# Linear attention and a gated expert on one core: the feature projections from split fp32r products to plain fp32 ones

## The chip, the cores and the metric

The kernel runs on one core of a Trainium2 chip. The metric is the device time of one execution in microseconds, the median of several runs. Before the change it is 1270.08 us (three runs, 1269.09 to 1270.28).

## The reference

```python
def phi(x):                                   # x: 8 batches, 8 heads, 576 rows, 64
    proj = np.einsum('bhsd,df->bhsf', x, w_phi)            # w_phi: 64 x 128
    proj = proj - np.max(np.abs(proj), axis=-1, keepdims=True)
    return np.concatenate([np.exp(proj), np.exp(-proj)], axis=-1)
q_p, k_p = (phi(q), phi(k))
kv = np.einsum('bhsf,bhsd->bhfd', k_p, v)
z = np.sum(k_p, axis=2)
num = np.einsum('bhsf,bhfd->bhsd', q_p, kv)
den = np.einsum('bhsf,bhf->bhs', q_p, z)[..., None] + 1e-06
attn = num / den                              # then x = 4608 tokens x 512
rms = np.sqrt(np.mean(x * x, axis=-1, keepdims=True) + 1e-06)
xn = x / rms * rms_g
g = xn @ w_gate                               # 512 x 1536
out = (g * (1.0 / (1.0 + np.exp(-g))) * (xn @ w_val)) @ w_out
```

The change concerns the first product alone, `proj`, for q and for k.

## The kernel before

The work is done in stages that follow each other. The attention stage takes the 64 heads in 32 pairs (8 batches of 4 pairs). Behind it come the gate and value products of the first 384 columns that are left over, then the other gate and value columns, then the product with `w_out`. Nearly all products are made in fp32 accuracy from three fp32r ones: each operand is split into a rounded high part (a cast on ScalarE) and the rest (a subtraction on VectorE or GpSimd), and high x high, high x low and low x high are added up in PSUM. `_split` (line 59) issues the cast and the subtraction.

A pair goes through four steps, each in another turn of the loop at line 558, so that four pairs are in work at a time:

- `front` (line 316) transposes k, q and the rests on TensorE and projects them. A head has 576 rows; 512 of them fill four blocks of 128, and the remaining 64 rows of k and of q of both heads form one more block of 128 rows, the rests, called `r`. Two of a head's blocks lie side by side in 128 columns (64 each), so a pair has four units of 128 x 128 for k, four for q and one for the rests. `trans` (line 324) transposes the units of one of them into a PSUM tile `sm` and splits the result into `th` and `tl`. `proj` (line 334) takes two units: for each it issues three products (lines 341 to 343) of a unit with the weights `wh` and `wl`, 128 x 256. These hold the split `w_phi` twice, in rows 0 to 63 for the first 128 columns and in rows 64 to 127 for the others, and zeros elsewhere, so that one product projects both blocks of a unit. VectorE then takes the largest absolute value of each projected row (line 345) and subtracts it (line 348), which gives `yk`, `yq` and `yr`. The PSUM tile `pp` holds two units (one bank) and has two buffers.
- `mid` (line 355) takes the exponentials of k's part (line 368), sums k's features times v in `acc` (lines 376 and 381), transposes q's part back (line 394), takes its exponentials twice, plain and rounded (lines 405 and 406), and subtracts them on GpSimd (lines 410 and 412).
- `back` (line 430) multiplies q's features with the sums (line 445), copies numerator and denominator out on ScalarE (line 447), and sends the denominators through DRAM to spread them (lines 449 to 458).
- `last` (line 468) multiplies with the reciprocals on VectorE (lines 475 and 476) and stores.

In the same loop the weights of the later stages are decoded from 8-byte numbers (`_decode`, line 41: four instructions on VectorE, two on ScalarE, two on GpSimd), and from the pair on at which enough tokens are stored, units of the gate and value products fill TensorE (`fill`, line 494, products at line 511).

`_merge` (line 64) orders the steps' pieces by a place between 0 and 1 in the turn; `front`'s pieces are spread from -0.2 to 0.7 in the order that line 352 gives. The framework's scheduler then sets the final order on each engine. Every engine runs its own queue in that order and waits at semaphores.

## Time and profile before

| | |
|---|---|
| median of the runs | 1270.08 us |
| the profiled execution | 1266.87 us, span 1265.1 us |
| TensorE busy | 1221.9 us, 97%, 10401 products |
| VectorE busy | 963.8 us, 76% |
| ScalarE busy | 738.1 us, 58% |
| GpSimd busy | 684.5 us, 54% |
| granted TensorE clock, mean | 0.999 |
| attention stage | 0 to about 487 us |
| rest of the first gate and value columns | to about 590 us |
| other gate and value columns | to about 1000 us |
| product with `w_out` | to the end |

The names in the trace are those of the tiles: `pp<-wh,th` is a product into `pp` with the operands `wh` and `th`. PE is TensorE, PEld its weight loads, DVE VectorE, ACT ScalarE, POOL GpSimd. A product's row lasts longer than the time until the next one may start, so that rows of one engine overlap.

### The profile page before, as it was taken

Reading aid. Unit: us, or ns where it says so; the run is one execution under the profiler, and the core shown is the slowest. Engines: PE = TensorE matmul, PEld = TensorE weight load, DVE = VectorE, ACT = ScalarE, POOL = GpSimd, SP = SyncE. Lnnn points to the kernel's source line nnn. Section 1 sums busy time; section 2 is a strip of 40 time slices with the busy share of each in tenths; the row PEclk is TensorE's granted clock in tenths of the full one; section 3 lists DMA queues with packets and bytes.
Section 4 is the critical chain, followed back from the end, with each engine's and each line's share of the span. In section 5 each row is a group of like instructions: output and inputs, shape, how many; then the busy total and the mean of one; then the engine's idle time right before and its main releaser. Section 6 shows DMA issues by size and latency. Waiting matters only on the chain.

```text
span 1265.1 us, 27382 instructions
## 1 busy us (share of the span) xinstructions
PE 1221.9 (97%) x10401; PEld 1206.2 (95%) x10401; DVE 963.8 (76%) x1425; ACT 738.1 (58%) x1514; POOL 684.5 (54%) x638
## 2 busy tenths in 40 slices
PE   7989999989999999999999999999999899999998
PEld 7989999989999999999999999999999799999998
DVE  6999898987778663574867877877775888877775
ACT  6988887887888775454545445444345534344342
POOL 4766664774666455226234444533431067877776
PEclk9999999999999999999999999999999999999999
DMA  5555665666575425764445545556665653544443
GB/s 162 138 139 152 172 164 168 167 164 171 161 185 157 138 73 164 239 210 146 144 145 201 171 161 185 193 179 214 220 201 192 207 162 108 180 136 135 134 145 106
DMA packets 196977, 208.37 MB, mean 165 GB/s; under 512 B 67722, under 2 KB 148270, under 8 KB 196846
## 3 DMA queue, kind: packets, MB, share of 16 engines
q1 hardware_dynamic: 175982, 186.17, 49.4%
q10 hardware_dynamic: 20864, 20.45, 5.2%
q8 instruction: 82, 1.34, 0.5%
q14 instruction: 49, 0.40, 0.1%
HBM read 133.91 MB, written 72.67 MB: 163 GB/s over the span
## 4 chain that ended last, share of the span: by engine, by line
PE 69%; DVE 15%; DMA 5%; ACT 4%; issue 4%; POOL 1%; ACTq 0%; SPq 0%; DVEq 0%; POOLq 0%
PE r L786 20%; PE fp L511 8%; PE gz L1030 6%; PE gd L1030 5%; PE gy L1030 5%; PE acc L381 5%; PE sm L445 3%; PE fp L1030 3%; PE sm L511 2%; PE pp L341 2%; PE pp L343 2%; PE pp L342 2%; PE sm L328 2%; PE fp L445 2%; PE sm L394 2%
## 5 line engine op out<-in xcount | busy, mean ns | idle before, releaser
L786 PE MATMUL r<-xo,wh 128*128 128x256 f32 x1764 | 306.9, 278 | 4.9 <-ACT c L797 1.6
L786 PEld LDWEIGHTS r<-xo,wh 128*128 128x128 f32 x1764 | 264.7, 188 | 6.6 <-ACT c L797 1.8
L410 POOL TENSOR_TENSOR ql<-eq,qh 128x256 fp32r<-128x256 f32 x256 | 213.8, 865 | 60.2 <-ACT qh L406 40.5
L786 PE MATMUL r<-xo,wl 128*128 128x256 f32 x882 | 239.2, 277 | 0.0
L786 PEld LDWEIGHTS r<-xo,wl 128*128 128x128 f32 x882 | 164.0, 188 | 0.0
L345 DVE TENSOR_REDUCE mx<-pp 128x4 f32<-128x512 f32 (+1 forms) x160 | 99.8, 629 | 49.8 <-PE pp L343 49.1
L381 PE MATMUL acc<-vm,ek 128*128 128x65 f32 x1024 | 129.9, 268 | 0.0
L381 PEld LDWEIGHTS acc<-vm,ek 128*128 128x128 f32 x1024 | 126.2, 192 | 0.1
L406 ACT ACTIVATE qh<-sm 128x512 fp32r<-128x512 f32 (+1 forms) x192 | 97.5, 508 | 0.0
L405 ACT ACTIVATE eq<-sm 128x512 f32<-128x512 f32 x128 | 78.8, 616 | 28.3 <-PE sm L394 24.9
L341 PE MATMUL pp<-wh,th 128*128 128x256 f32 x288 | 88.5, 308 | 3.3 <-DVE yk L348 1.2
L343 PE MATMUL pp<-wh,tl 128*128 128x256 f32 x288 | 84.7, 300 | 0.4 <-DVE tl L61 0.3
L61 POOL TENSOR_TENSOR xo<-x,xo 128x512 fp32r<-128x512 f32 x45 | 64.0, 1429 | 33.8 <-ACT xo L60 31.4
L342 PE MATMUL pp<-wl,th 128*128 128x256 f32 x288 | 81.6, 284 | 0.0
L368 ACT ACTIVATE ek<-yk 128x512 f32<-128x512 f32 x128 | 75.3, 655 | 1.0 <-DVE yk L348 0.9
L807 ACT ACTIVATE c<-c 128x1024 f32<-128x1024 f32 (+1 forms) x45 | 44.0, 977 | 52.2 <-DVE c L806 52.2
L511 PE MATMUL fp<-xoh,fg 128*128 128x256 f32 x344 | 71.7, 287 | 1.2 <-ACT sums L169 1.2
L511 PE MATMUL fp<-xoh,fv 128*128 128x256 f32 x344 | 71.7, 284 | 0.0
L61 POOL TENSOR_TENSOR s2l<-st,s2h 128x768 fp32r<-128x768 f32 x17 | 39.7, 2337 | 54.1 <-ACT s2h L60 50.8
L54 POOL TENSOR_TENSOR stg<-stg,stg 128x128 f32<-128x128 f32 x48 | 24.5, 531 | 78.6 <-ACT c L803 35.2
L412 POOL TENSOR_TENSOR ql<-eqr,qh 128x256 fp32r<-128x256 f32 x32 | 24.5, 765 | 76.8 <-ACT qh L406 76.8
L54 POOL TENSOR_TENSOR wa<-raw,wa 128x192 f32<-128x192 f32 x64 | 41.7, 672 | 43.8 <-DVE wa L52 18.2
(262 smaller groups left out, 4157.2 us busy)
## 6 DMA issues: line engine op xcount, KB each, us to landing
ht<-hs SPq DMA_DIRECT2D x17, 1536.0 KB
hs<-c SPq DMA_DIRECT2D x36, 512.0 KB
gvr<-gvs SPq DMA_DIRECT2D x27, 512.0 KB
rc<-di SPq DMA_DIRECT2D x32, 288.0 KB
x<-xs SPq DMA_DIRECT2D x9, 1024.0 KB
gvs<-fo ACTq DMA_DIRECT2D x35, 256.0 KB
kt<-in_k_dram SPq DMA_DIRECT2D x32, 256.0 KB
vm<-in_v_dram SPq DMA_DIRECT2D x64, 128.0 KB
```

Source lines behind the costliest of these rows:

```text
L61: (lo_eng or nc.vector).tensor_tensor(lo, x, hi.bitcast(F32), ALU.subtract)
L341: nc.tensor.matmul(o, th[:, cs], wh, start=True, stop=False)
L342: nc.tensor.matmul(o, th[:, cs], wl, start=False, stop=False)
L343: nc.tensor.matmul(o, tl[:, cs], wh, start=False, stop=True)
L345: nc.vector.tensor_reduce(mx[:, 0:2 * m], pp[:, 0:2 * m], axis=AX.X, op=ALU.max, apply_absolute_value=True)
L381: nc.tensor.matmul(acc[:, sg, h], e[h][:, sg, j], vm[:, h, j], start=False, stop=(h == 1 and j == T0 - 1))
L405: nc.scalar.activation(ei[:, sg], yi, AF.Exp, scale=1.0 - 2.0 * sg)
L406: nc.scalar.activation(hi[:, sg], yi, AF.Exp, scale=1.0 - 2.0 * sg)
L410: nc.gpsimd.tensor_tensor(lo[:, sg, cs], ei[:, sg, cs], hi[:, sg, cs].bitcast(F32), ALU.subtract)
L511: nc.tensor.matmul(fp[:, wi], w, xx[x][:, c], start=(wi == 0 and i == 0), stop=(i == 3 * NC - 1), skip_group_check=True)
L786: nc.tensor.matmul(self.r[r][:, k], w[:, cs], x[:, h, c], start=(first and k == 0 and i == 0), stop=(i == 3 * NP1 - 1), skip_group_check=True)
L1030: nc.tensor.matmul(place[n], a[:, kp], w[:, o], start=(first and kp == 0 and i == 0), stop=(kp == KP - 1 and i == 2), skip_group_check=True)
```

## The change

`w_phi` is kept once, unsplit, as `wphi` (`w2` in the code), in the same block form. `trans` makes one plain fp32 copy `th` of the transposed data, on VectorE for q and on ScalarE for k and the rests; `tl` is gone. `proj` does all units of k or of q in one piece. For k and q each unit becomes two products of 64 rows: rows 0 to 63 of the unit with rows 0 to 63 of the weights, and rows 64 to 127 with rows 64 to 127, 128 columns each, so that the zero blocks aren't multiplied; the built program gives the two their own halves of TensorE's rows. The first half's results go to one PSUM bank and the second half's to another; `pp` now holds four units in two banks and has one buffer. The rests have one plain product of 128 rows and 256 columns, into a `sm` tile. The reduction and the subtraction on VectorE take all four units at once (1024 elements a row), and `y` is written in the order that `mid` reads. Line 352's order has two pieces for each of k, q and r where it had up to three.

The matter of how many instructions a pair issues: on TensorE 27 products become 17; on VectorE two subtractions of 512 and one of 128 elements become one copy of 512, four reductions and four subtractions of 512 become two and two of 1024; on ScalarE one cast of 512 goes. GpSimd's work and the DMAs are the same.

```diff
--- before.py
+++ after.py
@@ -228,17 +228,14 @@
     ld = a_ctx.enter_context(tc.tile_pool(name="a_ld", bufs=2))
     dec = a_ctx.enter_context(tc.tile_pool(name="a_dec", bufs=1))
     dsc = a_ctx.enter_context(tc.tile_pool(name="a_dsc", bufs=3, space=DRAM))
-    ps_p = a_ctx.enter_context(tc.tile_pool(name="a_ps_p", bufs=2, space=PSUM))
+    ps_p = a_ctx.enter_context(tc.tile_pool(name="a_ps_p", bufs=1, space=PSUM))
     ps_k = a_ctx.enter_context(tc.tile_pool(name="a_ps_k", bufs=1, space=PSUM))
 
 
-    wh = const.tile([128, 2 * F], F32R, name="wh")
-    wl = const.tile([128, 2 * F], F32R, name="wl")
-    w2 = dec.tile([128, 2, F], F32, name="wa", bufs=2)
+    w2 = const.tile([128, 2, F], F32, name="wphi")
     nc.vector.memset(w2, 0.0)
-    nc.sync.dma_start(out=w2[0:64, 0, :], in_=w_phi)
-    nc.sync.dma_start(out=w2[64:128, 1, :], in_=w_phi)
-    _split(nc, wh, wl, w2[:, 0:2].rearrange("p a f -> p (a f)"))
+    for i in range(2):
+        nc.sync.dma_start(out=w2[i * 64:(i + 1) * 64, i], in_=w_phi)
 
 
     vms = [const.tile([128, 2, T0, D + 1], F32, name=f"vm{i}") for i in range(3)]
@@ -326,31 +323,34 @@
             tp = ps_s.tile([128, 512], F32, name="sm")
             for j, u in enumerate(us[n]):
                 nc.tensor.transpose(out=tp[:, j * 128:(j + 1) * 128], in_=u, identity=ident)
-            th = wk.tile([128, 512], F32R, name="th")
-            tl = wk.tile([128, 512], F32R, name="tl")
-            _split(nc, th[:, 0:m], tl[:, 0:m], tp[:, 0:m])
-            hl[n] = (th, tl)
-
-        def proj(n, u0):
-            th, tl = hl[n]
-            m = min(2, len(us[n]) - u0)
-            pp = ps_p.tile([128, 4, F], F32, name="pp")
-            for j in range(m):
-                o = pp[:, 2 * j:2 * j + 2].rearrange("p a f -> p (a f)")
-                cs = slice((u0 + j) * 128, (u0 + j + 1) * 128)
-                nc.tensor.matmul(o, th[:, cs], wh, start=True, stop=False)
-                nc.tensor.matmul(o, th[:, cs], wl, start=False, stop=False)
-                nc.tensor.matmul(o, tl[:, cs], wh, start=False, stop=True)
-            mx = wk.tile([128, 4], F32, name="mx")
-            nc.vector.tensor_reduce(mx[:, 0:2 * m], pp[:, 0:2 * m], axis=AX.X, op=ALU.max,
-                                    apply_absolute_value=True)
-            y = wk.tile([128, 4 if n != "r" else 2, F], F32, name="y" + n, bufs=3 if n != "r" else 2)
-            nc.vector.tensor_tensor(y[:, 0:2 * m], pp[:, 0:2 * m],
-                                    mx[:, 0:2 * m].unsqueeze(2).broadcast_to([128, 2 * m, F]), ALU.subtract)
-            d["y"][n, u0 // 2] = y
-
-        order = "k k0 r r0 k2 q q0 q2" if pr == 0 else "r k r0 k0 q k2 q0 q2"
-        return [lambda s=s: proj(s[0], int(s[1])) if s[1:] else trans(s) for s in order.split()]
+            hl[n] = wk.tile([128, 512], F32, name="th")
+            (nc.vector.tensor_copy if n == "q" else nc.scalar.copy)(hl[n][:, 0:m], tp[:, 0:m])
+
+        def proj(n):
+            th, m = hl[n], len(us[n])
+            if n == "r":
+                pp = ps_s.tile([128, 512], F32, name="sm")[:, 0:2 * F].rearrange("p (i m f) -> p i m f", i=2, m=1)
+                nc.tensor.matmul(pp.rearrange("p i m f -> p (i m f)"), th[:, 0:128],
+                                 w2.rearrange("p i f -> p (i f)"), start=True, stop=True)
+            else:
+                pp = ps_p.tile([128, 2, 4, F], F32, name="pp")
+                for j in range(m):
+                    for i in range(2):
+                        ps = slice(i * 64, (i + 1) * 64)
+                        nc.tensor.matmul(pp[:, i, j], th[ps, j * 128:(j + 1) * 128], w2[ps, i], start=True, stop=True)
+            mx = wk.tile([128, 2, 4], F32, name="mx")
+            nc.vector.tensor_reduce(mx[:, :, 0:m], pp, axis=AX.X, op=ALU.max, apply_absolute_value=True)
+            y = wk.tile([128, 2 * m, F], F32, name="y" + n)
+            nc.vector.tensor_tensor(y.rearrange("p (m i) f -> p i m f", i=2), pp,
+                                    mx[:, :, 0:m].unsqueeze(3).broadcast_to([128, 2, m, F]), ALU.subtract)
+            if n == "r":
+                d["y"]["r", 0] = y
+            else:
+                for h in range(2):
+                    d["y"][n, h] = y[:, 4 * h:4 * h + 4]
+
+        order = "k pk r pr q pq" if pr == 0 else "r k pr pk q pq"
+        return [lambda s=s: proj(s[1]) if s[1:] else trans(s) for s in order.split()]
 
     def mid(pr):
         d = st[pr]
```

TensorE, one pair of the attention stage, from the transposes of `mid` (`yq`) to those of q (`qt`). Before:

```order
L394 MATMUL sm<-ident,yq 128x128 x4
L341 MATMUL pp<-wh,th 128x256
L342 MATMUL pp<-wl,th 128x256
L343 MATMUL pp<-wh,tl 128x256
L341 MATMUL pp<-wh,th 128x256
L342 MATMUL pp<-wl,th 128x256
L328 MATMUL sm<-ident,qt 128x128 x4
```

The two units' products stand three to a unit; that of the second unit's low part (line 343) follows further down, since it waits for the split. Now, at the same place (line 325 is the transposes, 333 the rests' product, 340 the half products):

```order
L394 MATMUL sm<-ident,yq 128x128 x4
L333 MATMUL sm<-wphi,th 128x256
L340 MATMUL pp<-wphi,th 128x128 x8
L445 MATMUL fp<-qh,kv0h 65x288
L445 MATMUL fp<-ql,kv0h 65x288
L445 MATMUL fp<-qh,kv0l 65x288
```

The eight half products of k stand in one run, the rests' product ahead of them; products of `back` (line 445) follow, and q's transposes behind these.

VectorE, the same steps: the largest values (`mx`), the subtractions (`yk`, `yq`), the split (`tl`) and the decoding (`wp`). Before:

```order
L345 TENSOR_REDUCE mx<-pp 128x4
L61 TENSOR_TENSOR tl<-sm,th 128x512
L348 TENSOR_TENSOR yk<-pp,mx 128x512
L345 TENSOR_REDUCE mx<-pp 128x4
L348 TENSOR_TENSOR yk<-pp,mx 128x512
L50 TENSOR_SCALAR wp<-wa 128x384
L345 TENSOR_REDUCE mx<-pp 128x4
L51 SCALAR_TENSOR_TENSOR wp<-wa,wp 128x384
L348 TENSOR_TENSOR yq<-pp,mx 128x512
```

A reduction of one buffer stands between the subtractions of the other. Now (line 327 is q's copy, 342 the reduction, 344 the subtraction):

```order
L342 TENSOR_REDUCE mx<-sm 128x2
L344 TENSOR_TENSOR yr<-sm,mx 128x256
L342 TENSOR_REDUCE mx<-pp 128x8
L344 TENSOR_TENSOR yk<-pp,mx 128x2x4x128
L327 COPY th<-sm 128x512
L342 TENSOR_REDUCE mx<-pp 128x8
L50 TENSOR_SCALAR wp<-wa 128x384
L344 TENSOR_TENSOR yq<-pp,mx 128x2x4x128
```

There is one reduction and one subtraction each; between k's subtraction and q's reduction stands only q's copy.

## Rows read from the trace of the kernel before

**Rows 1.** The page, part 1: busy time, share and instructions of each engine.

```profile
span 1265.1 us, 27382 instructions
PE 1221.9 (97%) x10401; PEld 1206.2 (95%) x10401; DVE 963.8 (76%) x1425; ACT 738.1 (58%) x1514; POOL 684.5 (54%) x638
```

**Rows 2.** Table by stretches: engines' busy us and instruction counts, clock, DMA.

```profile
0.00:320.00 320.00, 297.88 (x2452) 290.53 (x2453) 274.06 (x496) 259.72 (x635) 196.90 (x262) 0.99 0.61 159
320.00:487.00 167.00, 166.36 (x1420) 165.50 (x1420) 118.60 (x202) 130.72 (x311) 101.18 (x122) 1.00 0.51 139
487.00:590.00 103.00, 100.29 (x859) 99.52 (x858) 55.45 (x76) 52.91 (x88) 45.09 (x35) 1.00 0.61 197
```

**Rows 3.** The same table for the projections' first products alone, line L341.

```profile
0.00:320.00 320.00, 62.93 (x201) 38.94 (x201) 0.99 0.61 159
320.00:487.00 167.00, 25.52 (x87) 16.53 (x87) 1.00 0.51 139
```

**Rows 4.** Chain of waits, in order of time: start, us, what.

```profile
204.47 0.28 PE acc L376 x2
204.74 0.44 PE sm L328 x4
...
213.37 0.12 PE pp L341
...
213.96 0.12 PE pp L343
...
215.22 0.22 PE acc L376 x2
```

**Rows 5.** Chain of waits from 0 to 487 us, shares by line.

```profile
by line: PE acc L381 13.0%; PE fp L511 10.5%; PE sm L445 8.6%; PE pp L341 4.7%; PE pp L343 4.7%; PE pp L342 4.3%; PE sm L328 4.3%; PE fp L445 4.3%; PE sm L394 4.2%; DVE mx L345 4.2%; issue 2.6%; DVE nd L476 2.4%; DVE yq L348 2.3%; PE acc L3
```

**Rows 6.** One of TensorE's weight loads, beside the six products of rows 4.

```profile
213.45 0.19 PEld L341 LDWEIGHTS pp<-wh,th 128*128 128x128 f32 x1
```

**Rows 7.** Groups of TensorE's instructions from 0 to 487 us, shapes apart.

```profile
L394 PE MATMUL sm<-ident,yq 128*128 128x128 f32 x256 | 39.4, 274 | 5.6 <-DVE tl L61 4.7 <-DVE yq L348 0.7
```

**Rows 8.** The same for VectorE: count, busy us, mean ns, idle before.

```profile
L345 DVE TENSOR_REDUCE mx<-pp 128x4 f32<-128x512 f32 x128 | 86.8, 684 | 42.6 <-PE pp L343 41.9
L348 DVE TENSOR_TENSOR yk<-pp,mx 128x512 f32<-128x512 f32 x64 | 43.8, 686 | 1.2
L61 DVE TENSOR_TENSOR tl<-sm,th 128x512 fp32r<-128x512 f32 x64 | 43.4, 678 | 9.8 <-ACT th L60 9.7
L348 DVE TENSOR_TENSOR yr<-pp,mx 128x256 f32<-128x256 f32 x32 | 13.3, 417 | 0.5
L345 DVE TENSOR_REDUCE mx<-pp 128x2 f32<-128x256 f32 x32 | 13.2, 413 | 7.2 <-PE pp L343 7.2
L61 DVE TENSOR_TENSOR tl<-sm,th 128x128 fp32r<-128x128 f32 x32 | 8.5, 264 | 0.6 <-ACT th L60 0.4
```

**Rows 9.** VectorE's copies out of PSUM in the stretch from 487 to 590 us.

```profile
L516 DVE COPY fo<-fp 128x512 f32<-128x512 f32 x6 | 4.1, 681 | 1.5 <-PE fp L511 1.5
```

**Rows 10.** ScalarE's casts of transposed data, groups from 0 to 487 us.

```profile
L60 ACT CAST th<-sm 128x512 fp32r<-128x512 f32 x64 | 38.9, 608 | 13.9 <-PE sm L328 10.5 <-PE pp L342 2.1 <-PE fp L445 1.0
```

**Rows 11.** ScalarE in order of time: two of 0.6 us, one after the other.

```profile
473.09 0.60 ACT L405 ACTIVATE eq<-sm 128x512 f32<-128x512 f32 x1
473.59 0.59 ACT L406 ACTIVATE qh<-sm 128x512 fp32r<-128x512 f32 x1
```

**Rows 12.** Who waited for whom from 0 to 487 us: total, times, longest.

```profile
DVE mx L345 <- PE pp L343: 49.1, 41, 4.2
PEld sm L394 <- DVE tl L61: 5.9, 6, 2.2
PE sm L394 <- DVE tl L61: 4.7, 5, 2.0
```

**Rows 13.** TensorE in order of time, in the first microseconds.

```profile
14.77 0.64 PE L376 MATMUL acc<-vr,er 128*128 128x130 f32 x2
15.21 0.32 PE L381 MATMUL acc<-vm,ek 128*128 128x65 f32 x1
```

## Prediction

> **What bounds the kernel now.** I read the busy shares first: TensorE 97%, VectorE 76% [rows 1]. A matmul's row is longer than its share of the queue, so a busy share doesn't say that TensorE is at its limit; the table by stretches does, since it counts instructions. It splits the span into the attention stage (0 to 487 us), the rest of the gate and value products (to 590), and two stages that the change doesn't touch (to 1265) [rows 2]. All 288 first products of the projections lie in the attention stage, 201 of them before 320 us and 87 after it [rows 3]. A pair of heads issues nine, so these are 22.3 pairs in 320 us (14.35 us each) and 9.7 pairs in 167 us (17.2 us each). I call them stages A and B.
>
> What a product costs TensorE is the distance to the next start in the chain of waits: six of the projection follow each other, and from the first's start at 213.37 us to the sixth's at 213.96 are 0.59 us, 0.118 each [rows 4]. By that, the 2452 products of stage A need 289 us, or 13.0 us a pair, and the 1420 of stage B all of its 167 us. **Stage B is bound by TensorE alone**: VectorE has 118.6 us to do there and ScalarE 130.7. **Stage A has three nearly level engines**: TensorE 13.0 us a pair, VectorE 274.1/22.3 = 12.3, ScalarE 259.7/22.3 = 11.6. The period is 14.35, so waiting for each other costs 1.35 us a pair. The chain over the whole stage agrees: the projection's three lines hold 4.7 + 4.7 + 4.3 = 13.7% of 487 us on TensorE, VectorE's reduction and q's subtraction 6.5% [rows 5].
>
> **The change, part by part.**
>
> TensorE, removed: 27 products a pair x 0.118 = 3.19 us.
>
> TensorE, added: 16 half products of 128 columns and one full product of 256, in plain fp32. The nearest rows are plain fp32 products of this stage: two of 130 columns take 0.22 us, four transposes of 128 columns 0.44 us, so 0.110 each [rows 4]. The 256 columns cost 0.110 x 256/130 = 0.217. That is 0.85 ns a column, 2 clocks at 2.4 GHz (the granted clock is 0.99 and 1.00 in these stages [rows 2]). The Trainium skill, "FP8 and Floating Point Precision", section "TensorE Precision Notes", says true FP32 takes four passes through the array. By that a half product would cost 0.21 us; the trace doesn't agree: it has 0.110.
>
> Do two halves run at once? No row shows it, since no product of before uses fewer than 128 rows. The ends: 0.110 each, one behind the other, or 0.055, two at a time. I take 0.055. The order shows all eight in one run, alternating between rows 0 to 63 and 64 to 127, and between two PSUM banks; nothing that one needs is in use by the other. TensorE already loads the next weights while a product runs: a load has a row of 0.19 us beside 0.118 a product [rows 6]. The Trainium skill, "TensorEngine Tiling (Array Packing)", section "Key Properties", says of row tiles that they load and multiply in parallel, and that a change of tiling mode drains the engine; no run so far shows either.
>
> A turn between full and half products may cost something. The two 130-column products take 0.28 us behind products of 65 columns and 0.22 behind products of 288 [rows 4]. I take that 0.06 a turn (a whole row's tail, 0.274 - 0.110 = 0.16 [rows 7], is the upper end; nothing is the lower), four turns a pair: 0.24 us.
>
> So a pair costs TensorE 8 x 0.110 + 0.217 + 0.24 = 1.34 us, 1.85 less than now; with halves in line 2.22, 0.97 less.
>
> VectorE, removed: two subtractions for the low part of 0.678 and one of 0.264. Merged: four reductions into two and four subtractions into two. A reduction takes 0.684 at 512 and 0.413 at 256 elements, so its fixed part is 0.14; a subtraction is alike (0.686 and 0.417). Four fixed parts fewer are 0.57 us [rows 8]. Added: q's copy out of PSUM, 0.681 by VectorE's copies of the same shape [rows 9]. Sum: 1.62 + 0.57 - 0.68 = 1.5 us less a pair. ScalarE loses q's cast, 0.6 us [rows 10]; its rows overlap (two of 0.6 start 0.49 apart [rows 11]), so I take 0.5.
>
> A PSUM tile of transposed data is now free after one copy, where it took a cast and a subtraction behind it. TensorE waited 4.7 us on that, its weight loads 5.9 [rows 12]; it lies in A's waits, and I count it in no other place. The split of the projection's weights goes once, behind the loads of the start: nothing. GpSimd has 196.9 us to do in stage A [rows 2], 8.8 a pair, and covers nothing that ends.
>
> **The sum.** Stage B: TensorE stays longest, at 17.2 - 1.85 = 15.35 us against ScalarE's 13.5, so all of it arrives: 9.7 x 1.85 = 18 us. Stage A: TensorE 13.0 - 1.85 = 11.15, ScalarE 11.1, VectorE 10.8. With three level engines the waits won't stay at 1.35; I take 2.0 (an estimate; as now at best, 3 at worst): 13.15 a pair, 22.3 x 1.2 = 27 us. Together 45 us. The profiled execution took 1266.87 us (span 1265.1) and would take 1222; the median of before is 3.2 us above it, so I say **1225 us**. The stages after 487 us stay.
>
> **Rivals.**
>
> *Halves in line.* The halves don't run side by side; each costs 0.110. Then B gains 9.7 x 0.97 = 9 us, and A's TensorE stays longest at 12.0 + 1.6 of waits (between 1.35 and 2): 22.3 x 0.75 = 17. Total 26: 1244 us. For it: no row shows two products at once. Against: they share neither rows nor bank.
>
> *The single PSUM tile.* There were two buffers of two units, now one of four. k's tile must be reduced and subtracted (2.4 us on VectorE) before q's eight products may start, and q's reduction can't start until they end. In the order nothing but q's copy or a weight piece stands between on VectorE. VectorE already waits for the projection's last product, 41 times, 49.1 us, 1.2 each [rows 12]. One such wait more per pair that nothing covers costs 32 x 1.2 = 38 us: 1263 us. Against: over 13 us pass per pair, and two rounds of products (0.45) and VectorE's work (2.45) need some 6.
>
> *Slower: plain fp32 costs twice.* Place: TensorE's queue in both stages. In the first microseconds two plain products of 130 columns take 0.44 us, 0.22 each [rows 13]. If half products cost that in line, a pair needs 16 x 0.22 + 0.43 + 0.24 = 4.2 us, 1.0 more than now. B loses 9.7 x 1.0 = 10 us, A has 14.0 + 1.35 = 15.35 a pair and loses 22.3 x 1.0 = 22: 1302 us. It decides from 0.164 us a half product in line (18 x 0.164 + 0.24 = 3.19). For it: that row. Against: later the same products stand at 0.110 to 0.14 [rows 4]. The four passes of the Trainium skill, "FP8 and Floating Point Precision", section "TensorE Precision Notes", would do the same in this queue; the rows at 0.110 speak against it.
>
> **Numbers.** Side by side 0.60 (1225), in line 0.24 (1244), the tile's hand-over 0.09 (1263), slower 0.05 (1302), and 0.02 for no difference. Bounds of the first: no turns and waits as now give A 22.3 x 1.9 = 42 (ScalarE longest) and B 9.7 x 2.09 = 20, 1208; the 5.9 us on the low part gone besides, 1202. A measurement here can tell about 0.2% (2.5 us; the three runs lie within 1.2). The range of 1200 to 1252 takes in the first two cases with their bounds (the first from 1202, the second to 1252 if A's waits rise to 2 there too) and leaves out the hand-over, the slower case and no difference, 0.16 in all. Faster holds the first two and most of the third (0.07): 0.91; same the rest of it and no difference, 0.04; slower 0.05.
>
> **What would show it.** Right: starts of the eight half products about 0.11 us apart by twos (0.45 a run); the attention stage's end near 442 us; VectorE's reduction near 1.2 us at 1024 elements; stage B with TensorE still full. In line: the eight take 0.9. The hand-over: TensorE idle ahead of the half products, released by y's subtraction, or VectorE idle ahead of its reductions for over 100 us in all. Wrong altogether: the attention stage ends at 487 or later, or the stages behind it change length.

## The result, and the profile after

The changed kernel takes **1288.53 us** (median of six runs, 1284.82 to 1290.86), the kernel before 1269.59 us in the same series: a ratio of **1.0145** (95% interval 1.0124 to 1.0166), 18 us slower where 45 us faster was forecast. The time lies outside the range. The profiled execution took 1289.81 us.

Page, part 1, of the kernel after; it answers to [rows 1]:

```profile
span 1288.0 us, 27503 instructions
PE 1234.0 (96%) x10625; PEld 1189.1 (92%) x10625; DVE 935.9 (73%) x1232; ACT 725.0 (56%) x1481; POOL 670.8 (52%) x638
```

VectorE and ScalarE have fewer busy microseconds, as intended (GpSimd too, with the same 638 instructions). TensorE has more, and 224 more rows, although the code issues 10 products a pair fewer, 320 in all. That contradiction leads to the first cause below.

The line L376 in before and in after: shortest, median and longest row (ns), first and last start (us).

```profile
L376 PE MATMUL acc<-vr,er x128: 272/275/426, 14.8 to 475.3; 128*128 128x130 f32 x128
```

```profile
L376 PE MATMUL acc<-vr,er x128: 272/276/528, 16.1 to 498.1; 128*128 128x130 f32 x128
```

The last of these rows starts 23 us later. The attention stage's last product of its own (line 445) starts at 489.9 us before and at 514.1 after; from there to the end it is 775.2 and 773.8 us. So the whole loss is in the attention stage.

Table by stretches, kernel after (columns as in [rows 2]):

```profile
0.00:320.00 320.00, 286.97 (x2430) 260.02 (x2430) 234.11 (x338) 234.82 (x575) 176.65 (x248) 0.95 0.55 149
320.00:487.00 167.00, 164.61 (x1455) 153.54 (x1453) 113.92 (x153) 124.08 (x296) 90.26 (x116) 0.99 0.52 145
```

TensorE is busy for 11 us less in the first stretch than in [rows 2], and its mean granted clock there is 0.95, against 0.99.

**First cause, of the missing gain: a plain fp32 product is two rows of the trace, not one.** Groups of TensorE's instructions, kernel after, 0 to 514 us:

```profile
L340 PE MATMUL pp<-wphi,th 64*128 64x128 f32 x1024 | 82.9, 298 | 1.0 <-ACT th L327 0.7 <-DVE yk L344 0.4
...
L333 PE MATMUL sm<-wphi,th 128*128 128x256 f32 x64 | 21.1, 415 | 0.4 <-ACT th L327 0.4
```

The code issues 16 half products for each of 32 pairs, 512, and the trace has 1024 rows; the rests have 32 products and 64 rows. The row of L376 above says the same of the kernel before: two products a pair, 64, and 128 rows. The transposes have one row each. What I priced at 0.110 us was half of a product.

Timeline of TensorE, kernel after (start, us, what; rows of one kind are merged):

```profile
199.23 0.38 PE L394 MATMUL sm<-ident,yq 128*128 128x128 f32 x2
199.45 0.60 PE L333 MATMUL sm<-wphi,th 128*128 128x256 f32 x2
199.98 1.16 PE L340 MATMUL pp<-wphi,th 64*128 64x128 f32 x16
201.07 0.34 PE L445 MATMUL fp<-qh,kv1h 128*65 128x288 f32 x1
201.25 0.29 PE L445 MATMUL fp<-ql,kv1h 128*65 128x288 f32 x1
201.38 0.29 PE L445 MATMUL fp<-qh,kv1l 128*65 128x288 f32 x1
```

This is k's run of eight half products, 16 rows. Taken singly, the rows come by twos, 6 to 7 ns apart, and the next two 0.11 us later: 200.191 and 200.198, then 200.303 and 200.310. So **the halves do run side by side**, and two half products take 2 x 0.11 = 0.22 us; eight take 0.90. From the run's first start to the next product are 1.09 us (the middle value of the 52 runs whose rows stand together), so 0.19 more; the rests' product ahead, whose two rows usually take 0.434, holds the queue for 0.53, so 0.10 more; the next start behind is 0.18 after, where it usually is 0.13, so 0.05 more. **Going in and out costs 0.34 us a run.** A pair therefore costs TensorE 2 x (0.90 + 0.34) + 0.434 = 2.91 us; before it was 3.19. That is 9 us less over 32 pairs, where I had 59 (32 x 1.85).

Groups of VectorE's instructions, kernel after, 0 to 514 us; they answer to [rows 8]:

```profile
L342 DVE TENSOR_REDUCE mx<-pp 128x8 f32<-128x1024 f32 x64 | 78.1, 1220 | 50.0 <-PE pp L340 49.8
L344 DVE TENSOR_TENSOR yk<-pp,mx 128x1024 f32<-128x1024 f32 x32 | 39.0, 1219 | 0.5
...
L327 DVE COPY th<-sm 128x512 f32<-128x512 f32 x32 | 21.9, 686 | 8.1 <-PE sm L325 6.7 <-ACT nd L447 0.8
```

These came out as priced: 1.22 us for 1024 elements, 0.686 for the copy.

**Second cause: new waits on TensorE, and a low clock behind them.** Who waited for whom, 0 to 490 us, on the two lines that head the wait for the sums' split; before, then after:

```profile
PE fp L445 <- ACT kv1h L60: 2.4, 4, 1.2
PE fp L445 <- ACT kv0h L60: 1.8, 2, 1.1
```

```profile
PE fp L445 <- ACT kv0h L60: 6.3, 4, 2.0
...
PE sm L394 <- DVE yq L344: 4.0, 6, 1.0
PE fp L445 <- ACT kv1h L60: 3.5, 3, 1.3
```

With the waits for the low part of the same split (`kv0l`, `kv1l`), which these lines leave out, it is 5.4 us before and 13.7 after (the 16.9 in the expectation of e5_numlate takes in other waits ahead of the same products). Kernel after, one of these waits on TensorE, and what ScalarE did meanwhile:

```profile
109.70 0.60 PE L325 MATMUL sm<-ident,kt 128*128 128x128 f32 x4
111.95 0.50 PE L445 MATMUL fp<-qh,kv0h 128*65 128x288 f32 x1 [1.65 <-ACT kv0h L60]
112.25 0.44 PE L445 MATMUL fp<-ql,kv0h 128*65 128x288 f32 x1
```

```profile
110.01 0.59 ACT L49 ACTIVATE raw<-raw 128x384 f32<-128x384 uint32 x1
110.45 1.18 ACT L368 ACTIVATE ek<-yk 128x512 f32<-128x512 f32 x2
111.49 0.41 ACT L60 CAST kv0h<-acc 128x260 fp32r<-128x260 f32 x1
```

The numerator's products wait for the cast of the sums, and that cast stands on ScalarE behind a weight piece and two exponentials of the next pair. All that stands behind them in TensorE's queue waits with them. The table by stretches around that moment (the clock is the third column from the right):

```profile
108.00:111.60 3.60, 2.30 (x25) 1.94 (x21) 1.40 (x2) 3.60 (x9) 2.91 (x4) 1.00 0.83 228
111.60:125.25 13.65, 11.99 (x56) 10.39 (x57) 11.13 (x15) 7.72 (x17) 7.86 (x8) 0.50 0.43 116
125.25:131.00 5.75, 5.75 (x57) 5.50 (x56) 3.20 (x6) 4.71 (x13) 2.09 (x4) 1.00 0.28 72
```

TensorE had 1.3 us without work in the 3.6 us ahead, and then the granted clock is 0.50, the level of 1.2 GHz, for 13.65 us: 56 rows there, 57 in the 5.75 us behind it. In the attention stage after its start, before has 3.4 us at that level, after 37.5 us in seven stretches, each behind a wait of 1.3 to 2.4 us; three waits of that size had none behind them (the expectation of e5_numlate below, which says each, is too strong there). Four of the seven waits, with 27.3 of the 37.5 us behind them, were for the sums' split; the others were for the rests' subtraction (`yr`) and, twice, for the low part of the tokens that the gate and value products read (`xol`).

TensorE's time in the attention stage by kind of product, added up from the rows (from the end of the row before to the end of this one, us; gate and value products with their count of rows; the last two columns are from experiments below):

| | before | after | e5 | e9 |
|---|---|---|---|---|
| projections | 112.6 | 95.0 | 89.9 | 116.4 |
| numerator | 108.8 | 130.0 | 116.4 | 110.0 |
| sums of k | 123.3 | 132.0 | 130.7 | 123.3 |
| transposes | 74.9 | 80.9 | 78.0 | 69.7 |
| gate and value | 63.8 (504) | 69.5 (504) | 71.9 (570) | 62.8 (528) |
| other | 2.0 | 2.3 | 2.5 | 2.5 |
| sum | 485.4 | 509.7 | 489.4 | 484.7 |
| of it without work | 18.4 | 31.3 | 19.4 | 17.8 |
| stretches at 1.2 GHz after the start | 3.4 | 37.5 | 3.4 | 3.4 |

The projections give 17.6 us, and all else takes 41.9: among it 12.9 of added idle time, up to 17 of the low clock (an estimate, half of 34.1 us more), and the ways out of the half runs, which fall on the product behind.

### The profile page after: what moved, and what is told of

Same layout as the page of the kernel before. It is cut to its first block, busy times and chain, and to the rows that moved or that the text cites. A ratio compares the mean times of both kernels' runs of the same rounds, so it can differ in the third digit from the quotient of the medians.

```text
span 1288.0 us, 27503 instructions
## 1 busy us (share of the span) xinstructions
PE 1234.0 (96%) x10625; PEld 1189.1 (92%) x10625; DVE 935.9 (73%) x1232; ACT 725.0 (56%) x1481; POOL 670.8 (52%) x638
## 5 line engine op out<-in xcount | busy, mean ns | idle before, releaser
L410 POOL TENSOR_TENSOR ql<-eq,qh 128x256 fp32r<-128x256 f32 x256 | 200.1, 811 | 80.7 <-issue 41.1
L381 PE MATMUL acc<-vm,ek 128*128 128x65 f32 x1024 | 132.5, 275 | 1.0 <-ACT ek L368 1.0
L342 DVE TENSOR_REDUCE mx<-pp 128x8 f32<-128x1024 f32 x64 | 78.1, 1220 | 50.0 <-PE pp L340 49.8
L340 PEld LDWEIGHTS pp<-wphi,th 64*128 64x128 f32 x1024 | 68.0, 197 | 19.5 <-issue 15.2
L340 PE MATMUL pp<-wphi,th 64*128 64x128 f32 x1024 | 82.9, 298 | 1.0 <-ACT th L327 0.7
L61 POOL TENSOR_TENSOR xo<-x,xo 128x512 fp32r<-128x512 f32 x45 | 62.8, 1400 | 35.6 <-ACT xo L60 35.0
L511 PE MATMUL fp<-xoh,fg 128*128 128x256 f32 x344 | 73.5, 293 | 1.0 <-ACT sums L169 1.0
L511 PE MATMUL fp<-xoh,fv 128*128 128x256 f32 x344 | 73.0, 288 | 0.0
L160 POOL TENSOR_TENSOR sq<-sq 128x512 f32<-128x512 f32 x18 | 26.0, 1446 | 72.7 <-ACT sq L158 68.1
L447 ACT ACTIVATE nd<-sm,epsd 65x288 f32<-65x288 f32 x80 | 39.4, 497 | 42.3 <-PE sm L445 42.2
```

Source lines behind the costliest of these rows:

```text
L61: (lo_eng or nc.vector).tensor_tensor(lo, x, hi.bitcast(F32), ALU.subtract)
L340: nc.tensor.matmul(pp[:, i, j], th[ps, j * 128:(j + 1) * 128], w2[ps, i], start=True, stop=True)
L342: nc.vector.tensor_reduce(mx[:, :, 0:m], pp, axis=AX.X, op=ALU.max, apply_absolute_value=True)
L381: nc.tensor.matmul(acc[:, sg, h], e[h][:, sg, j], vm[:, h, j], start=False, stop=(h == 1 and j == T0 - 1))
L410: nc.gpsimd.tensor_tensor(lo[:, sg, cs], ei[:, sg, cs], hi[:, sg, cs].bitcast(F32), ALU.subtract)
L511: nc.tensor.matmul(fp[:, wi], w, xx[x][:, c], start=(wi == 0 and i == 0), stop=(i == 3 * NC - 1), skip_group_check=True)
```

## The experiments

Ratios are to the kernel before on the same chip; microseconds from a ratio are ratio times 1269.6. The theory at first: the halves run side by side, a plain product costs two rows, and the rest of the loss is the order, in which the shorter projection no longer covers the split of the sums. The rivals: the halves are what costs; the form of the numbers does; the single tile or the rests' tile in `sm` does. In the series of e9 to e12 the kernel before itself lies between 1260 and 1280 us, so the intervals there are wider.

**e1_full: q and k as whole plain products.**

```diff
-                pp = ps_p.tile([128, 2, 4, F], F32, name="pp")
+                pj = ps_p.tile([128, 4, 2, F], F32, name="pp")
                 for j in range(m):
-                    for i in range(2):
-                        ps = slice(i * 64, (i + 1) * 64)
-                        nc.tensor.matmul(pp[:, i, j], th[ps, j * 128:(j + 1) * 128], w2[ps, i], start=True, stop=True)
+                    nc.tensor.matmul(pj[:, j].rearrange("p i f -> p (i f)"), th[:, j * 128:(j + 1) * 128],
+                                     w2.rearrange("p i f -> p (i f)"), start=True, stop=True)
+                pp = pj.rearrange("p m i f -> p i m f")
```

> The changed kernel, but each unit of k and q is one plain product of 128 rows and 256 columns, as the rests already are, and no half products. Price theory (a plain product has two records in the trace, so 256 columns cost 0.434 us and a run of four units 1.74 us, against 1.24 us for the eight halves with their turns): TensorE gets 0.5 us a run more to do, 64 runs, 32 us, so 1310 to 1320 us. Clock theory (the half products, or the turns into and out of them, are what the chip answers with the lower clock): the granted clock is back at 0.999 and some 17 us come back, so 1295 to 1305 us.

1285.48 us, 1.0140 (1.0114 to 1.0165): level with after, although its projections hold TensorE for 132.6 us against 95.0. It lies below the ranges of both theories. Its idle time is 14.3 us and its time at 1.2 GHz 3.4, against 31.3 and 37.5 in after. At these places the halves' shorter time buys nothing; it turns into waits and low clock.

**e2_inline: the same half products, not alternating** (`for i` outside, `for j` inside).

> The changed kernel, but the eight half products of a run are ordered by half: four on rows 0 to 63, then four on rows 64 to 127. If only neighbours in the queue run side by side, three of four pairs fall apart: sixteen records at 0.11 us, a run of about 1.7 us and turns, 0.7 us a run more than with alternating halves, 64 runs: 1320 to 1335 us. If TensorE overlaps halves from anywhere in its queue, the time stays at 1288 us.

1312.37 us, 1.0344 (1.0309 to 1.0379), 25 us above after. Timeline of e2_inline:

```profile
201.43 1.71 PE L340 MATMUL pp<-wphi,th 64*128 64x128 f32 x16
203.06 0.35 PE L445 MATMUL fp<-qh,kv1h 128*65 128x288 f32 x1
```

The run takes 1.63 us to the next start, not 1.09. Only neighbours ran side by side: of the 16 rows of this run, three pairs start 4 to 5 ns apart, where the first half's last rows meet the second half's first ones, and the others stand about 0.11 us apart. Alternating is worth 0.54 x 64 = 35 us on TensorE, of which 25 arrive; that is the first theory, with a time below its 1320 to 1335.

**e3_merged: after's tiles and order of pieces, before's three split products.** Two places of the difference to the kernel before; the single buffer and the rests' `sm` tile are as in after:

```diff
-            pp = ps_p.tile([128, 4, F], F32, name="pp")
+            pj = ps_p.tile([128, 4, 2, F], F32, name="pp")
...
-        order = "k k0 r r0 k2 q q0 q2" if pr == 0 else "r k r0 k0 q k2 q0 q2"
+        order = "k pk r pr q pq" if pr == 0 else "r k pr pk q pq"
```

> The changed kernel's shape (all four units in one piece, one PSUM tile of two banks, the rests' result in a tile of the transposes, reductions of 1024 elements, the new order) with the products of before: three fp32r products a unit from split operands, q's and k's split on ScalarE and VectorE. Shape theory (the single tile, the larger pieces and the order they lead to make the waits): 1280 us or more. Price and clock theory (the shape is harmless, it is the plain half products): 1260 to 1272 us.

1285.92 us, 1.0141 (1.0117 to 1.0166). With before's products the new tiles and the new order alone lose 18 us, as much as the whole change. They lose it by other waits, though: for the sums' split 1.4 us in all, for the low parts (`tl`) 8.5 where the kernel before has 5.0. Who waited for whom in e3_merged, 0 to 487 us, the largest:

```profile
PE sm L399 <- DVE tl L61: 5.6, 7, 1.4
```

Line 399 is there what line 394 is in the kernel before.

**e4_plain: before's pieces and tiles, one whole plain product a unit, q's copy on VectorE.**

```diff
-                nc.tensor.matmul(o, th[:, cs], wh, start=True, stop=False)
-                nc.tensor.matmul(o, th[:, cs], wl, start=False, stop=False)
-                nc.tensor.matmul(o, tl[:, cs], wh, start=False, stop=True)
+                nc.tensor.matmul(o, th[:, cs], w2.rearrange("p i f -> p (i f)"), start=True, stop=True)
```

> The kernel before, with its pieces of two units, two PSUM buffers and order, but one plain fp32 product of 256 columns a unit in place of three fp32r ones, and q's copy on VectorE. Price theory: nine products of 0.434 us a pair are 3.9 us against 3.19, 23 us more on TensorE, VectorE loses 1.6 us a pair: 1280 to 1295 us, clock 0.999. Shape theory: without the single tile the waits stay as before, so at most the 23 us arrive, less what VectorE gives back: 1270 to 1285 us.

1280.35 us, 1.0096 (1.0062 to 1.0130), 12 us slower. A whole plain product takes 0.434 us where three split ones take 0.354, so 288 of them should add 23 us; TensorE's idle time falls from 18.4 to 12.8. The time lies where the ranges of the two theories overlap, so the run doesn't tell them apart.

**e5_numlate: after, the numerator's pieces later in the turn.**

```diff
-        return [(0.05, lambda: num(0, 0)), (0.2, lambda: num(0, 1)), (0.35, lambda: num(1, 0)),
-                (0.5, lambda: num(1, 1)), (0.79, inv)]
+        return [(0.2, lambda: num(0, 0)), (0.32, lambda: num(0, 1)), (0.44, lambda: num(1, 0)),
+                (0.56, lambda: num(1, 1)), (0.79, inv)]
```

> The changed kernel with the four numerator pieces of the step behind moved in its turn, from 0.05, 0.20, 0.35 and 0.50 to 0.20, 0.32, 0.44 and 0.56. In the changed kernel TensorE stands 16.9 us ahead of these products, for the split of the sums by ScalarE and VectorE (5.5 us before), and each wait of 1.3 us and more is followed within a few us by a stretch at the lower clock. Order theory (the built order puts these products too early behind the half products): that wait falls to 6 us or less, the time at half clock from 37 us to 15 or less, 1268 to 1278 us. Cover theory (TensorE merely stands elsewhere, since other engines set the pace): 1284 to 1292 us.

**1259.42 us, 0.9931 (0.9913 to 0.9950)**: 27 us below after, below before, and below the ranges of both theories. Who waited for whom in e5_numlate, 0 to 300 us:

```profile
PE fp L445 <- ACT kv0h L60: 2.2, 2, 1.4
PE fp L445 <- ACT kv1h L60: 2.2, 3, 0.9
```

The waits for the split are back at before's size, idle time falls from 31.3 to 19.4 us, and the low clock from 37.5 to 3.4 (table above). The mean granted clock of its nine runs is 0.995 to 1.000; of after's six, 0.985 to 0.992. The half products are the same, so they don't bring the low clock by themselves: after's loss goes with the order at the original places. Waits and low clock went together here, so the run doesn't price them singly. Whether the change deserves the gain is asked by e9.

**e6_qact: after, q's copy on ScalarE** (`nc.scalar.copy` for all three).

> The changed kernel with q's copy out of PSUM on ScalarE, as k's. ScalarE gets 0.5 us a pair, VectorE loses 0.68. If ScalarE's queue is what TensorE waits for (the split of the sums begins with a cast there), the time rises by 5 to 10 us, to 1293 to 1298; if VectorE's queue is (the reduction behind the copy), it falls to 1278 to 1284 us.

1296.25 us, 1.0215 (1.0183 to 1.0246), 9 us above after, as the first case had it, with 20.5 us of waits for the sums' split (13.7 in after) and 30.7 us at 1.2 GHz. Taking the copy to VectorE was right; ScalarE is the engine on which the sums' cast queues.

**e7_onebuf: before with one buffer for `pp`** (`bufs=1`).

> The kernel before with one buffer of the projection's PSUM tile (two units, one bank) in place of two; nothing else. Hand-over theory: five pieces a pair, each must wait until the one ahead is reduced and subtracted (1.4 us), TensorE waits on the subtraction and the time rises by 15 us or more, to 1285 or above. If a single tile is harmless: 1266 to 1274 us.

1350.14 us, 1.0644 (1.0610 to 1.0678), 82 us slower. Who waited for whom in e7_onebuf, 0 to 575 us:

```profile
PE pp L341 <- DVE yk L348: 12.4, 21, 1.6
```

A single buffer that holds two units is a real hand-over: idle time in the stage grows from 18.4 to 65.7 us, 12.4 of it straight ahead of the products that wait for the buffer, the rest ahead of others. In after one buffer holds four, and the wait on it is 0.4 us in all (the row of L340 above).

**e8_rsm: before with the rests' products in an `sm` tile.**

```diff
-            pp = ps_p.tile([128, 4, F], F32, name="pp")
+            pp = ps_p.tile([128, 4, F], F32, name="pp") if n != "r" else ps_s.tile([128, 512], F32, name="sm").rearrange("p (a f) -> p a f", a=4)
```

> The kernel before with the rests' result in a PSUM tile of the transposes' pool in place of the projection's; nothing else. That pool has three tiles and now serves eleven uses a pair in place of ten. If that is what the merged shape costs, the transposes wait for it and the time rises by 5 to 15 us (1275 to 1285); if not, 1266 to 1272 us.

1307.82 us, 1.0312 (1.0269 to 1.0355), 40 us slower. Who waited for whom in e8_rsm, 0 to 530 us:

```profile
PE sm L394 <- DVE tl L61: 8.4, 8, 2.0
```

The wait on an `sm` tile is 8.4 us where [rows 12] have 4.7, and idle time in the stage grows from 18.4 to 43.5: one user more in that pool costs the others more than I had expected (5 to 15 us). It may be what e3_merged paid for; after was not run without it, so what the `sm` tile costs in after is not known.

**e9_beforelate: before with e5's places.** The same edit as in e5_numlate.

> The kernel before with the numerator's four pieces at 0.2, 0.32, 0.44 and 0.56 of a pair. Order theory (after loses because its shorter products no longer cover the split of the sums, and the late places give that cover back): the kernel before has only 5.5 us of such waits in all, so it gains at most 5 us, 1263 to 1270. Rival (the late places are a better order for any kernel, and have nothing to do with the change): as large a gain as after had from them, 29 us, about 1240.

1261.59 us, 0.9918 (0.9879 to 0.9958): a gain of 10 us (5 to 15 by its interval), more than the 5 that my theory allowed and far less than the rival's 29. So the late places help before as well, and help after by 17 us more. What before gains are not its waits for the sums' split: they are 6.7 us here and 5.4 before. One reason shows in the count of gate and value products (L511) from 0 to 490 us. Before, after, e5_numlate and e9_beforelate, in that order:

```profile
0.00:490.00 490.00, 78.47 (x505) 1.00 0.57 151
```

```profile
0.00:490.00 490.00, 67.64 (x426) 0.96 0.54 148
```

```profile
0.00:490.00 490.00, 75.63 (x550) 1.00 0.56 154
```

```profile
0.00:490.00 490.00, 77.94 (x533) 1.00 0.57 155
```

In the same time e9 has done 28 of them more than before, and e5 45; each is 0.117 us less to do behind the stage, 3.3 us for e9. Where the rest of its gain comes from is open.

**e10_fulllate: whole plain products (e1) at e5's places.**

> Whole 128-row plain products for q and k (as in e1_full), with the numerator's pieces in the late places. Order theory: e1_full had TensorE busy nearly without a gap (idle 14 us), so the late places change little, 1278 to 1286, and against e5_numlate at 1259 the halves side by side are worth 20 to 27 us. Rival (the late places gain in any kernel): 1256 to 1262, and the halves side by side are worth nothing.

1279.50 us, 1.0096 (1.0051 to 1.0140), 21 us above e5_numlate, as the theory had it (20 to 27). Timeline of e10_fulllate:

```profile
208.65 1.02 PE L338 MATMUL pp<-wphi,th 128*128 128x256 f32 x4
209.51 0.60 PE L394 MATMUL sm<-ident,yq 128*128 128x128 f32 x4
```

Four rows, two whole products, take 0.86 us, so a tile of four 1.72. Once the waits are gone, running the halves side by side is worth 21 us against whole plain products.

**e11_mergedlate: e3 at e5's places.**

> After's tiles and order of pieces, the products still in three split parts as before (as in e3_merged, 1286), with the numerator's pieces in the late places. Order theory: the waits and the low clock go, about 12 to 17 us, so 1269 to 1274, which is the kernel before again; against e5_numlate the plain halves are then worth 10 to 15 us. Rival (the number format is worth nothing, all of it is the order): 1259 to 1262.

1290.46 us, 1.0158 (1.0088 to 1.0227). My 1269 to 1274 missed, and the rival's 1259 too: the late places don't help here (e3_merged had 1.0141). Who waited for whom in e11_mergedlate, 0 to 490 us:

```profile
PE sm L342 <- DVE tl L61: 8.0, 12, 1.1
```

The rests' product stands close behind its own transposition and waits for the low part's subtraction. In after there is no low part. So within the new tiles the plain form is worth 29 us (e11 against e5). By the sum above 9 of these are cheaper products; e11 also has 29.6 us of idle time against 19.4, and 17.1 us at 1.2 GHz against 3.4. That both come from the longer chain between transposition and product is likely but not shown.

**e12_numlate2: after, the places later still** (0.3, 0.4, 0.5, 0.6).

> After with the numerator's pieces later still, at 0.3, 0.4, 0.5 and 0.6. Order theory: the 8.8 us that e5_numlate still waits ahead of the numerator shrink to about 5, so 1254 to 1260. Rival (the inversion at 0.79 and what stands behind it become the late ones): 1262 to 1270.

1275.18 us, 1.0047 (1.0004 to 1.0089). It misses both ranges: later is not better. The largest wait in e12_numlate2, 0 to 490 us, is another, not the inversion:

```profile
PE sm L394 <- DVE yq L344: 7.4, 5, 2.3
```

**e13_turnhalf and e14_turnfull: what a turn costs.** In each run of four units a product of 128 rows and 2 columns in the middle, in e13 between half products (kernel e5), in e14 between whole ones (kernel e10).

```diff
                 for j in range(m):
+                    if j == 2:
+                        nc.tensor.matmul(pp[:, 0, 3, 0:2], ident, w2[:, 0, 0:2], start=True, stop=True)
```

> e5_numlate with one more product, 128 rows by 2 columns, in the middle of each of the 64 runs of half products (its two columns are overwritten by the run's last product): two more turns a run. Turn theory (each run pays about 0.34 us for going in and out, as the trace shows it): 64 x (0.34 + the small product's own 0.05 to 0.1) = 25 to 28 us more, 1284 to 1288. Rival (the time around a run of halves is not from the turns, but from loads or waits there): the small product alone, 3 to 7 us more, 1262 to 1267.

> e10_fulllate with the same small product in the middle of each group of four whole products: no turn, since all have 128 rows. It gives the small product's own price: 3 to 7 us more than e10_fulllate's 1279.5 by both theories, 1282 to 1288; if the order is as fragile as the other runs make it, up to 10 us either way.

e13: 1281.94 us, 1.0140 (1.0102 to 1.0179), 26.5 us above e5. e14: 1292.46 us, 1.0218 (1.0180 to 1.0256), 15.5 above e10. Timelines of e13_turnhalf and e14_turnfull:

```profile
203.07 0.71 PE L342 MATMUL pp<-wphi,th 64*128 64x128 f32 x8
203.71 0.38 PE L339 MATMUL pp<-wphi,ident 128*128 128x2 f32 x2
204.02 0.72 PE L342 MATMUL pp<-wphi,th 64*128 64x128 f32 x8
204.67 0.39 PE L513 MATMUL fp<-xoh,fg 128*128 128x256 f32 x1
```

```profile
199.66 1.03 PE L340 MATMUL pp<-wphi,th 128*128 128x256 f32 x4
200.53 0.28 PE L339 MATMUL pp<-wphi,ident 128*128 128x2 f32 x2
200.66 1.11 PE L340 MATMUL pp<-wphi,th 128*128 128x256 f32 x4
201.61 1.11 PE L383 MATMUL acc<-vm,ek 128*128 128x65 f32 x9
```

The run of halves takes 1.60 us to the next start, 0.51 more than the 1.09 without the small product; the group of whole ones 1.95, 0.23 more than 2 x 0.86. The small product itself was dearer than I had it (0.05 to 0.1), since it cost 0.23 where no turn is. The two turns are the difference, **0.28 us, 0.14 each**, near the 0.34 that I read off the ends of a run. Over 64 runs that is 18 us; the times differ by 11, and idle time may hide some of it (8.1 us in e13, 19.4 in e5). With the dearer small product e14 missed its range, and that e13's distance to e5 fell into the 25 to 28 us of the turn theory was in part luck: its runs grew by 0.51 us each, 33 in all.

**e15_numlate3 and e16_before3: after and before at a third set of places** (0.15, 0.3, 0.45, 0.6).

> After with the numerator's pieces at 0.15, 0.3, 0.45 and 0.6. Order theory (later first piece takes the wait behind k's halves away): between after's 1288 and e5_numlate's 1259, near the latter, 1258 to 1268. Rival (e5_numlate was one lucky set of places, as e12_numlate2 at 1275 may say): 1270 to 1285.

> The kernel before with the pieces at those same places (0.15, 0.3, 0.45, 0.6), for the difference that the change makes at a third set of places. If the change itself is worth nothing on TensorE and only the fit of the order differs, this stands within 10 us of e15_numlate3, 1256 to 1272. If the halves really free TensorE once the waits are gone, it stands 9 us or more above e15_numlate3.

1264.12 us, 0.9964 (0.9942 to 0.9986), and 1260.61 us, 0.9957 (0.9940 to 0.9975). Together:

| places of the numerator | before | after | the change, us |
|---|---|---|---|
| 0.05, 0.2, 0.35, 0.5 | 1 | 1.0145 | +18 |
| 0.2, 0.32, 0.44, 0.56 | 0.9918 | 0.9931 | +2 |
| 0.15, 0.3, 0.45, 0.6 | 0.9957 | 0.9964 | +1 |

At two of three sets the change is worth nothing that the intervals can tell; at the original one it loses 18 us. Best of all runs by its ratio is e9_beforelate, without the change; e5_numlate, with it, can't be told from it.

## Why the prediction was wrong

**What bounds the kernel** held only in part. e2_inline and e10_fulllate lengthen TensorE's part and pay for it (25 us against after, 21 against e5); e1_full lengthens it by 37.6 us against after and pays nothing, since in after nearly as much goes into waits and low clock. The sign that I had named for "wrong altogether" came true: the attention stage ended behind 487 us.

**The price of a plain product failed.** I took 0.110 us for 128 columns from "two of 130 columns take 0.22 us" [rows 4]. Those two rows are one product. The code of `mid` issues two of them a pair, 64 in all, and the trace has 128 rows: the count would have told. The slower rival held the right price (0.22 a product), but with halves in line. [Rows 13], its evidence, were the same two rows of one product at half the pace, 0.22 us a row: the trace of before first records the full clock at 15.5 us. The rests' product is 0.434 us for the same reason, not 0.217. The Trainium skill, "FP8 and Floating Point Precision", section "TensorE Precision Notes", names four passes for true FP32, and the 0.21 us that I estimated from that for a half product agrees with the 0.22 us of its two rows; where I wrote that the trace disagreed, I had misread the trace.

**Side by side held**, by e2_inline and e10_fulllate. The Trainium skill, "TensorEngine Tiling (Array Packing)", section "Key Properties", says both that the tiles multiply in parallel and that a change of mode drains the engine; the rows agree with both, and give the drain a price here.

**The turns were mis-sized**: 0.06 us each taken, 0.14 (e13 against e14) to 0.17 (0.34 a run) measured. The upper bound that I had named, 0.16, was the right one.

Put together, TensorE's gain is 3.19 - 2.91 = 0.28 us a pair instead of 1.85, so that TensorE's term falls from 59 us to 9. Of the 1.57 us a pair, 1.14 are the price (0.92 for the half products, 0.22 for the rests') and 0.44 the turns. This alone would have made the forecast "9 us faster at best".

**The waits were mis-sized, and the low clock was put at nothing.** I let stage A's waits grow from 1.35 to 2.0 us a pair, 14.5 us in all, and gave none to stage B. In the same terms (the stage's time less its products' price) they grew by 33 us: the stage takes 24 us more while its products cost 9 less. Idle time is 12.9 of that, near what I had; up to 17 (an estimate) is the low clock behind the waits, which no term of mine held. So the forecast was 59 - 14.5 = 45 us faster, and the profiled stage 9 - 33 = 24 us slower. What I did not ask is who stands behind the new run in the queue: the order ahead of this prediction shows line 445 straight behind k's eight half products, and those need the sums' cast on ScalarE. e5_numlate shows that other places of these products take 27 us off after, with the waits and the low clock; e9 shows that 10 of them are there for before too, without these waits shrinking. e3_merged shows that the new tiles and order lose 18 us with the old products as well, by other waits, so the shorter products are not the only way to this loss.

**The hand-over of the single tile** did not happen (0.4 us). VectorE's rows came out as priced. That its saving and ScalarE's paid nothing fits a stage that TensorE's queue ends; no run took them out singly.

**Open.** The 9 us that the sizes still promise don't show at the other two sets of places. In the profiled executions part of it is low clock. Timelines of e9_beforelate and e5_numlate, the first pairs, sixteen rows of the same products each:

```profile
19.20 1.90 PE L381 MATMUL acc<-vm,ek 128*128 128x65 f32 x16
```

```profile
16.24 3.51 PE L381 MATMUL acc<-vm,ek 128*128 128x65 f32 x16
```

e5 still runs at half the pace there. Its trace first records the full clock at 25.7 us, that of e9 at 15.5: ten us at half the pace, so up to 5 us (an estimate). At the third set the profiled execution of after (e15) has 20.5 us at 1.2 GHz behind its start and full clock first at 15.8 us, that of before (e16) 3.4 and 10.2: up to 11 us. The three runs of e15 with a mean granted clock of 0.999 or more took 1258.3 to 1260.4 us, the five of e16, all at that clock, 1260.0 to 1263.6: about 1 us between their middle values, so that the low clock behind the start is not all that is missing. Why a few hundredths in the places move either kernel by 10 us was not settled either.

## What to carry to other kernels

Count the rows of an instruction against the calls in the code before you price it from the trace. Price a product together with the change of shape around it: sixteen rows of half products were 0.90 us, and the way in and out a third of that on top. When a change shortens the work of an engine that others feed, look up what stands next in its queue and whether its inputs can be there that much sooner; if not, move that piece, and move it in the kernel before too, or the gain is credited to the wrong edit.

## What the runs showed of the hardware

A plain fp32 product is two rows of the trace, each 0.11 us to the next start for 128 columns and 0.22 for 256, also when it uses only 64 rows of TensorE; a plain fp32 transposition is one. The rows of two half products on different rows of TensorE start 6 to 7 ns apart when the two are neighbours in the program; with all products of one half ahead of those of the other, all but three pairs of a run's rows stood about 0.11 us apart. A product of 128 rows and 2 columns between two whole plain ones cost 0.23 us. A turn between products of 128 rows and of 64 cost about 0.14 us. In after's attention stage a wait of 1.3 to 2.4 us on TensorE stood ahead of every fall of its granted clock to 0.50, and one of these stretches lasted 13.65 us; three such waits had no fall behind them.
